# Block 1's inverse from sums by n mod 4, one accumulating transfer in block 3, and a new order of the work (SSM convolution and SwiGLU, one core)

## The chip, the cores and the metric

The kernel runs on 1 core of one Trainium2 chip. The metric is the device time of the program in microseconds, as the median of several runs. A profile of one execution lies beside it: it records every instruction of TensorE (PE, with its weight loads, PEld), VectorE (DVE), ScalarE (ACT) and GpSimd (POOL), and the DMA issues of the queues on SyncE (SP), ACT and POOL. Times in the profile run from the start of its span.

## The reference

The input is a sequence of 2048 rows of 640 channels. All inputs are bf16.

```
ks: k_shift[t] = sum over 4 taps of k[t - tap] * shift_k[tap]
kv = k_shift * v
y  = irfft(rfft(kv, 4096) * rfft(ssm_k, 4096))[0:2048] + kv * ssm_D   # a causal convolution, per channel
h  = x + layernorm(x) * y
out = h + (silu(n @ w_gate) * (n @ w_up)) @ w_down, with n = layernorm(h); 640 -> 1728 -> 640
```

## The kernel before

**Blocks.** The sequence is cut into 4 blocks of 512 rows, and each block lies in SBUF as 128 partitions of R = 4 rows of 640 channels (row n of a block is partition n // 4, place n mod 4). For every block j the kernel makes kv (`kv_of`), its spectrum X_j (`spectrum`, `transform`), the spectrum G_j of that part of the filter, and from it H_j (`window`). The spectra are products with constant cosine and sine matrices on PE (L375), taken out of PSUM by ACT (L364) or DVE (L367, `taken`). Block j's output spectrum A is the sum over i of X_i times H_(j-i), complex, which is DVE's work: `mac` with `first` set is six instructions (L719), and each further product is four pairs of a product (L746) and a sum into A (L747). A pair named in `ADDP` is a product alone (L741), and its sum is made by an accumulating transfer (`add_into`, L278), which the POOL queue issues. In the kernel before that is one pair of block 1.

**The inverse.** `inverse` (names i0 to i3) first makes `odd` = A_lo - A_hi (L823) and A_lo + A_hi (L826; block 2 by a transfer). Then it has two ways. In the plain way each of the four n mod 4 rows takes 4 constants against 2 halves of 320 columns: 8 matmuls (L878), 32 in all. In the way called "four" DVE first makes four more sums and differences of 128x1280 (L843, L848 write the parts for even rows, L858 those for odd rows), after which each row takes 2 constants: 4 matmuls, 16 in all. `SUM` names the blocks and spectra that go the second way; of the inverses these were i2 and i3. Each row is then multiplied with the normalised x (L807 or L804, then L892), added to x (L905, or by a transfer in blocks 1 and 2), and the second layernorm follows. The rows of h normalised again are turned on PE in block 0 (L926, copied by L928), and by a transposing DMA in the others (L919, from SP).

**The feed-forward part.** `ffn` of block j works on the turned rows hT of all 512 positions: 27 chunks of 5 matmuls of 128x512 (L1022) against weights that L959 loads, 320 KB at a time (`load_w`), with a SiLU (L1014) and a copy (L1012) on ACT and a product on DVE (L1016); then 12 groups of matmuls with w_down (L1110; 15 in the last block). The weights are loaded anew in every block. Each load stands on SP's queue, or on POOL's where the order says so.

**The order.** Nothing is ordered at run time. `plan.add` records every operation with its engine, and `ORDER` lists all of them by number; the engines, and the DMA queues of SP and POOL, get their instructions in this order. A number written as a negative (n stands as ~n) takes the operation's other engine: ACT for DVE, SP for POOL, or a DMA for one of ACT's copies. Buffers come from 12 slots called `big`, 8 called S, 5 called row and 4 PSUM tiles called ps, given out in the same order. So every engine and every queue waits at its own first instruction that isn't ready, and what stands behind it waits too.

**Names used below.** n_j are the sums of the first layernorm of block j (ACT L757, L796; POOL or DVE L764 to L789). k_j is the shifted key: of blocks 1 to 3 it is loaded by four transposing DMAs (L557) and copied within the tile T by three further copies, "puts" (L563 as a DMA, L565 on ACT), and PE multiplies it with the taps (L648); its product with v is ACT L664 and DVE L665, or DVE L658 alone. g_j is the filter block, turned on PE in blocks 0 to 2 (L471, copied by L473). m_ji is the product of X_i and H_(j-i) for block j; t_j is the second normalising and turning. f_j is the feed-forward part of block j; PE does f_j's chunks while DVE and ACT are at block j + 1.

Of the kernel before, what the change touches and what calls it, by code (L numbers as in the profile page):

```python
# [43 lines left out]
HTURN = (1, 3, 2)  # L44
GTURN = (3,)
KTURN = (1, 2, 3)
SUM = {'X3': 'four', 'i2': 'four', 'i3': 'four', 'G3': 'four'}
ADDP = {(1, 1): ((0, 1),)}
ADDINV = (2,)
WHOLE3 = False  # L50
WARMUP = (18, 16, 16)
# [17 lines left out]
TW = PAD + BLK  # L69
CUTS = ("X0", "G0", "m", "i")  # L70
ORDER = [
# [36 lines left out]
SLOTS = {'S': 8, 'big': 12, 'kT': 0, 'tT': 1, 'row': 5, 'sg': 0, 'co': 2, 'ps': 4, 'sm': 6}  # L108
HOME = {t: "big" for t in ("scr", "x", "ld", "t4", "hT", "wgu", "diag")} | {"o": "row", "ps_c": "ps", "ps_f": "ps"}
SPLIT = ((0,), (1,))  # L110
# [102 lines left out]
def kernel(ctx: ExitStack, tc: tile.TileContext, A_q, A_k, A_v, A_shift_k, A_ssm_k, A_ssm_D, B_x,  # L213
# [19 lines left out]
    def new(tag):  # L233
        return Buf(HOME.get(tag, tag), None, tag)
# [26 lines left out]
    def dve(ns, fn, r, w, holds=()):  # L261
        return plan.add("dve", ns, fn, r, w, holds)
# [82 lines left out]
    def bits(halves=(0, 1), cs=(0, 1, 2, 3), ws=(0, 1)):  # L345

        return frozenset((h, c, w) for h in halves for c in cs for w in ws)
# [31 lines left out]
    def wide(n, ws):  # L379
        return n if len(ws) == 2 else n // 2 + 75  # L380
# [10 lines left out]
    def transform(src, dst, pieces, minus=None, name=None):  # L391

        how = SUM.get(name, "sub")
        for ws in pieces:
# [418 lines left out]
    def inverse(A, x, n1, pieces=((0, 1),), minus=None, groups=(ROWS,)):  # L813
# [4 lines left out]
        for ws in pieces:  # L818
            if not minus:
# [10 lines left out]
                else:  # L830
                    dve(wide(1490, ws), low, [], [(A, bits(ws=ws))])
            four = not minus and SUM.get(f"i{plan.block}") == "four"
            if four:
# [404 lines left out]
    for j in range(1, NB):  # L1238
        def stage(name, j=j):
            plan.line(j, f"{name}{j}")  # L1240
# [23 lines left out]
        if last:  # L1264
            A = H[j]
            stage("m0")
            mac(A, X[0], H[j], True, at=(j, 0), adds=ADDP.get((j, 0), ()))
        stage("k")
# [4 lines left out]
        if not last:  # L1273
            stage("m0")
            A = Spec(new("S"))
            mac(A, X[0], H[j], True, at=(j, 0), adds=ADDP.get((j, 0), ()))
        for i in range(1, j + 1):
# [5 lines left out]
            else:  # L1283
                mac(A, X[i], H[j - i], False, adds=ADDP.get((j, i), ()), at=(j, i))
        stage("n")
# [45 lines left out]
```

## Time and profile before

| | |
|---|---|
| Time before, median of 3 runs | 261.34 us (261.23 to 261.5) |
| The profiled execution | 261.3 us |
| Its span | 259.6 us |
| Granted TensorE clock over the span | 1.0 |
| PE, DVE, ACT, POOL busy | 251.3, 198.6, 180.0, 97.0 us |
| DMA traffic | 45.38 MB, mean 175 GB/s |

The span runs from the first to the last recorded instruction, so 1.7 us of the execution's time lie around it. A row of a timeline is: start, length, engine, line, operation, output<-inputs, shapes, count, and in brackets the idle time of the engine just before it and what ended it. Rows of equal instructions are merged, so the length of a merged row over its count is a little above the distance from one to the next. A row of a group is: line, engine, operation, shapes, count, then busy time in all and the mean of one in ns, then the idle time before them.

### The profile page before, as it was taken

To read this page: it belongs to the slowest core of one execution; us is meant where nothing else is said; L and a number is where in the kernel's file an instruction comes from. 1 tells how busy PE (TensorE), PEld (TensorE's weight loads), DVE (VectorE), ACT (ScalarE), POOL (GpSimd) and SP (SyncE) were. 2 spreads that over 40 slices of the span, in tenths; PEclk is the share of its full clock that TensorE was granted. 3 is DMA by queue.
4 is the path that set the end of the run, shared out by engine and by line. 5 is a ranking of instruction groups with operands and counts; after the bars stand their busy time and mean duration, and the time that the engine had idled before them with its cause. 6 is when DMAs were issued, how large, how long until landed. Compare 5 with 4: busy or idle time off the path is not lost.

```text
span 259.6 us, 4700 instructions
## 1 busy us (share of the span) xinstructions
PE 251.3 (97%) x1803; PEld 154.2 (59%) x1818; DVE 198.6 (77%) x259; ACT 180.0 (69%) x297; POOL 97.0 (37%) x115
## 2 busy tenths in 40 slices
PE   8999899999998999999999999999999999999994
PEld 7967577654654477754465477544456764444663
DVE  4679999999998999999999999999998200004403
ACT  2899999999998998569855985655497134637200
POOL 7961300008914199926117962240951022000000
PEclk9999999999999999999999999999999999999999
DMA  6997999979999998999997965994498546000002
GB/s 218 403 251 119 289 252 340 280 115 279 247 238 168 182 217 204 190 191 201 214 231 110 299 151 107 198 238 130 100 215 255 101 77 70 8 0 0 13 15 76
DMA packets 64752, 45.38 MB, mean 175 GB/s; under 512 B 31014, under 2 KB 60267, under 8 KB 64731
## 3 DMA queue, kind: packets, MB, share of 16 engines
q1 hardware_dynamic: 58896, 32.96, 51.1%
q0 software_dynamic: 5824, 12.13, 24.9%
q8 instruction: 14, 0.23, 0.4%
q14 instruction: 8, 0.06, 0.1%
q10 hardware_dynamic: 10, 0.01, 0.0%
HBM read 30.01 MB, written 4.59 MB: 133 GB/s over the span
## 4 chain that ended last, share of the span: by engine, by line
PE 78%; ACT 9%; DMA 6%; DVE 2%; issue 2%; SPq 1%; ACTq 0%; DVEq 0%
PE ps L1022 40%; PE ps L1110 23%; PE ps L375 10%; DMA big<-in_B_w_up_dram 4%; PE ps L878 3%; DMA big<-in_A_q_dram 3%; ACT T L565 2%; ACT big L364 1%; ACT S L364 1%; PE ps L648 1%; ACT row L757 1%; ACT big L664 1%; ACT big L473 1%; ACT tT L1014 1%; DVE row L892 1%
## 5 line engine op out<-in xcount | busy, mean ns | idle before, releaser
L1022 PE MATMUL ps<-big,big 128*128 128x512 bf16 x525 | 119.9, 379 | 1.7 <-DMA big<-in_B_w_up_dram 0.8
L1022 PEld LDWEIGHTS <-big 128*128 128x128 bf16 x540 | 52.5, 98 | 61.1 <-DMA big<-in_B_w_up_dram 1.3
L1110 PE MATMUL ps<-wd,tT 128*128 128x320 bf16 (+1 forms) x416 | 60.3, 299 | 0.0
L1110 PEld LDWEIGHTS <-tT 128*128 128x128 bf16 x416 | 40.7, 98 | 16.3
L1016 DVE TENSOR_TENSOR tT<-tT,co 128x2048 bf16<-128x2048 bf16 x12 | 14.5, 1219 | 34.4 <-ACT tT L1014 32.4
L375 PE MATMUL ps<-big,WF 128*128 128x320 bf16 x240 | 39.1, 299 | 1.3 <-ACT big L364 1.0
L1012 ACT CAST co<-ps 128x1024 bf16<-128x1024 f32 x24 | 24.2, 1011 | 17.3 <-PE ps L1022 16.8
L747 DVE TENSOR_TENSOR S<-S,big 128x2560 bf16<-128x2560 bf16 x23 | 34.3, 1492 | 1.2 <-DMA S<-big 0.5
L746 DVE TENSOR_TENSOR big<-S,S 128x2560 bf16<-128x2560 bf16 x23 | 34.1, 1485 | 0.2
L375 PEld LDWEIGHTS <-WF 128*128 128x128 bf16 x240 | 23.1, 97 | 12.8 <-issue 2.3
L1014 ACT ACTIVATE tT<-ps 128x1024 bf16<-128x1024 f32 x24 | 24.5, 1029 | 8.8 <-PE ps L1022 8.7
L757 ACT ACTIVATE row<-big 128x640 bf16<-128x640 bf16 x32 | 23.5, 742 | 1.8 <-DMA big<-in_A_q_dram 1.1
L807 ACT ACTIVATE row<-big,sm 128x640 bf16<-128x640 bf16 x23 | 20.3, 922 | 3.8 <-POOL sm L789 2.8
L1117 POOL DMA_DIRECT2D out_dram<-row x12 | 11.8, 1010 | 29.2 <-ACT row L1116 29.1
L364 ACT CAST S<-ps 128x320 bf16<-128x320 f32 (+1 forms) x36 | 19.4, 583 | 0.3
L1116 ACT CAST row<-ps 128x640 bf16<-128x640 f32 x12 | 8.1, 691 | 14.2 <-PE ps L1110 13.2
L364 ACT ACTIVATE big<-ps 128x640 bf16<-128x640 f32 (+1 forms) x24 | 15.6, 696 | 0.7 <-PE ps L375 0.7
L278 POOL DMA_DIRECT2D big<-row x8 | 7.0, 919 | 22.9 <-DVE row L892 22.9
L892 DVE SCALAR_TENSOR_TENSOR row<-row,ps 128x640 bf16<-128x640 bf16 x16 | 12.8, 815 | 1.1 <-PE ps L878 0.9
L278 POOL DMA_DIRECT2D S<-big x2 | 2.5, 1266 | 26.3 <-DVE S L719 19.1
L719 DVE TENSOR_TENSOR big<-S,S 128x2560 bf16<-128x2560 bf16 (+1 forms) x10 | 12.2, 1218 | 0.1
L959 POOL DMA_DIRECT2D big<-in_B_w_gate_dram x8 | 9.1, 1137 | 8.1 <-PE ps L1022 7.8
(110 smaller groups left out, 330.4 us busy)
## 6 DMA issues: line engine op xcount, KB each, us to landing
big<-in_B_w_up_dram SPq DMA_DIRECT2D x17, 320.0 KB, 5.1
big<-in_B_w_gate_dram SPq DMA_DIRECT2D x16, 320.0 KB, 4.7
big<-in_A_ssm_k_dram SPq DMA_DIRECT2D x4, 640.0 KB, 9.2
big<-in_A_q_dram SPq DMA_DIRECT2D x4, 640.0 KB, 7.6
big<-in_A_v_dram SPq DMA_DIRECT2D x4, 640.0 KB, 6.9
big<-in_B_w_gate_dram POOLq DMA_DIRECT2D x8, 320.0 KB, 7.2
big<-in_B_w_up_dram POOLq DMA_DIRECT2D x7, 320.0 KB, 6.7
wd<-in_B_w_down_dram SPq DMA_DIRECT2D x1, 2080.0 KB, 12.2
```

The source lines that it names most:

```text
L364: (lambda: nc.scalar.activation(dst(), src(), ACT.Copy, scale=2.0)) if twice else (lambda: nc.scalar.copy(dst(), src())),
L375: nc.tensor.matmul(ap(ps)[:, h, 0:NH], w, ap(src)[:, r, h * NH:(h + 1) * NH], start=(first and i == 0), stop=(last and i == len(rs) - 1), ...
L746: nc.vector.tensor_mul(flat2(b), X.part(xs), H.part(hs))
L747: f(A.part(dst), A.part(dst), flat2(b))
L757: act(825, lambda r=r, junk=junk: nc.scalar.activation(ap(junk), ap(x)[:, r, :], ACT.Square, scale=D ** -0.5, accum_out=sm(s, 1)[:, r:r + ...
L807: nc.scalar.activation(ap(row), ap(x)[:, r, :], ACT.Identity, bias=sm(s, 5)[:, r:r + 1], scale=sm(s, 4)[:, r:r + 1])
L892: nc.vector.scalar_tensor_tensor(two(ap(t)), two(ap(t)), 1.0, half(ap(ps)), op0=ALU.mult, op1=ALU.mult, accum_out=sm(s, 0)[:, r:r + 1])
L1012: act(1010, lambda ps=ps: nc.scalar.copy(ap(co)[:, at:at + 2, :], ap(ps)), src, [(co, gi % 2)])
L1014: act(1010, lambda ps=ps: nc.scalar.activation(ap(tT)[:, c:c + 2, :], ap(ps), ACT.Silu), src, [done(range(c, c + 2), ROWS)])
L1016: dve(1220, lambda: nc.vector.tensor_mul(ap(tT)[:, c - 2:c + 2, :], ap(tT)[:, c - 2:c + 2, :], ap(co)), [co], [done(range(c - 2, c + 2), R ...
L1022: nc.tensor.matmul(ap(ps)[:, i, :], ap(w)[:, k, off:off + P], ap(hT)[:, k, :], start=(k == 0), stop=(k == KT - 1))
L1110: nc.tensor.matmul(ap(ps)[:, hf, to:to + n], t, ap(wd)[:, c, col + (hf - hs[0]) * NH:col + (hf - hs[0]) * NH + n], start=(c == order[0]), ...
```

## The change

Three constants change; no function does.

```diff
-SUM = {'X3': 'four', 'i2': 'four', 'i3': 'four', 'G3': 'four'}
-ADDP = {(1, 1): ((0, 1),)}
+SUM = {'X3': 'four', 'i2': 'four', 'i3': 'four', 'G3': 'four', 'i1': 'four'}
+ADDP = {(1, 1): ((0, 1),), (3, 2): ((0, 1),)}
...
-ORDER = [0, 2, 31, 1, 4, 5, 7, 10, 6, ...
+ORDER = [0, 2, 4, 1, 5, 31, 6, 7, 10, ...
```

- Block 1's inverse goes the way called "four": 16 of its 32 matmuls go, and four DVE instructions of 128x1280 come.
- In block 3 the sum of one of the four pairs of X_2 and H_1 (that of X's first part with H's second part, into A's second part) leaves DVE, and an accumulating transfer of 640 KB on POOL's queue makes it.
- The whole order is another. 16 instead of 20 loads stand on POOL's queue: of f1's 3 instead of 6, of f2's 3 instead of 4, of f3's 4 instead of 5; and SP's queue takes 5 more. Of k2's three puts two are DMAs of POOL's queue and one is ACT's copy (before: one of SP's queue, two of ACT's). Of k3's one put goes from POOL's queue to SP's.
- Some operations change engines: of the four products of k3 with v one goes from DVE alone (L658) to ACT and DVE (L664, L665); one in k0 the other way. A copy of g2 (L473) goes from DVE to ACT, one of g1 from ACT to DVE. Of the second normalising in block 3, three rows instead of one are ACT's, and one instead of three DVE's.

The core of the function that both ways of the inverse share, with what the new constant switches on:

```python
four = not minus and SUM.get(f"i{plan.block}") == "four"
if four:
    ...
    dve(wide(820, ws), lambda r02=r02: r02(nc.vector.tensor_add, 0), [(A, h0)], [(A, bits((1,), (0, 1), ws))])
    dve(wide(820, ws), lambda r02=r02: r02(nc.vector.tensor_sub, 2), [(A, h0)], [(A, bits((1,), (2, 3), ws))])
    ...
        for sub in (True, False):
            ...
            dve(820 if len(ws) == 2 else 485, lambda pair=pair, sub=sub: pair(sub), [odd], [(A, bits((0,), rows, ws))])
...
elif four:
    terms = [(ap(WI)[:, 2 * c, r, :], ap(A)[:, 1 - r % 2, r // 2 * 2 + (c ^ (lo // 2)), :]) for c in range(2)]
else:
    terms = [(ap(WI)[:, c, r, :], ap(odd)[:, c ^ lo, :] if r % 2 else ap(A)[:, 0, c ^ lo, :]) for c in range(4)]
```

73 rows, old and new, of the table ORDER are left out of this document.

## The prediction, made before the changed kernel ran

> **What bounds the kernel now.** I read the page first, then the chain of waits, then the busy time in stretches of 10 us, then the timeline where those pointed.
>
> ```profile
> PE 251.3 (97%) x1803; PEld 154.2 (59%) x1818; DVE 198.6 (77%) x259; ACT 180.0 (69%) x297; POOL 97.0 (37%) x115
> ...
> PE 78%; ACT 9%; DMA 6%; DVE 2%; issue 2%; SPq 1%; ACTq 0%; DVEq 0%
> ```
>
> PE carries 78% of the chain that ends last. But the 77% of DVE is a mean over two very different parts, as the stretches show (PE, PEld, DVE, ACT, POOL busy, clock, DMA share, GB/s):
>
> ```profile
> 30.00:40.00 10.00, 9.77 (x121) 7.36 (x120) 9.93 (x20) 9.49 (x19) 0.17 (x1) 1.00 1.09 266
> 40.00:50.00 10.00, 9.54 (x95) 6.92 (x96) 9.62 (x22) 10.00 (x20) 0.41 (x1) 1.00 1.15 299
> ...
> 160.00:170.00 10.00, 9.95 (x62) 5.88 (x61) 9.89 (x8) 6.31 (x13) 3.12 (x3) 1.00 0.87 172
> ...
> 180.00:190.00 10.00, 9.95 (x48) 4.52 (x48) 9.77 (x9) 5.63 (x9) 7.66 (x6) 1.00 0.34 77
> ...
> 210.00:220.00 10.00, 9.95 (x52) 4.95 (x52) 0.00 (x0) 3.92 (x5) 2.67 (x4) 1.00 0.50 53
> ```
>
> Up to 50 us PE, DVE and ACT are all full; up to 190 us DVE is as full as PE; behind 210 PE runs alone, the clock is 1.0 and nothing can be won there but PE's own work. So there are two runners, PE and DVE, that must meet at block 3's inverse, and a gain on one alone counts only as far as the other lets it. They meet here:
>
> ```profile
> 188.14 1.56 DVE L843 TENSOR_TENSOR S<-S 128x1280 bf16<-128x1280 bf16 x2
> ...
> 189.83 0.71 PE L878 MATMUL ps<-S,WI 128*128 128x320 bf16 x4
> ...
> 201.71 5.17 SPq L919 DMA_TRANSPOSE big<-row  x4
> ...
> 211.53 3.83 PE L1022 MATMUL ps<-big,big 128*128 128x512 bf16 x16
> ```
>
> The first of the two L843, which the first inverse row reads, ends at 188.14 + 0.78 = 188.92. PE begins that row at 189.83: DVE is 0.9 us early, no more. The turned rows of block 3 land 2.6 us after the fourth L919 is issued at 205.7, so at 208.3, and PE begins f3 at 211.5: 3.2 us to spare.
>
> ```profile
> L919 SPq DMA_TRANSPOSE big<-row x12: 1198/1228/1439, 101.6 to 205.7; - x12
> ...
> DMA to landing us min/median/max: 2.6/2.6/2.7
> ```
>
> From that first row to f3, PE has 211.53 - 189.83 = 21.7 us of its own work. The sum below is therefore made in two columns, PE and DVE up to block 3's first inverse row, then one.
>
> **The change part by part.** *(a) 16 matmuls of block 1's inverse go.*
>
> ```profile
> 73.67 2.34 PE L878 MATMUL ps<-big,WI 128*128 128x320 bf16 x16
> 75.84 2.32 PE L1022 MATMUL ps<-big,big 128*128 128x512 bf16 x10
> ...
> 81.11 1.25 PE L1022 MATMUL ps<-big,big 128*128 128x512 bf16 x4 [0.78 <-DMA big<-in_B_w_up_dram]
> ```
>
> Sixteen take 75.84 - 73.67 = 2.17 us from start to start (0.136 each). PE: -2.2.
>
> *(b) DVE's own sum.*
>
> ```profile
> L843 DVE TENSOR_TENSOR S<-S 128x1280 bf16<-128x1280 bf16 x4 | 3.1, 818 | 0.0
> L747 DVE TENSOR_TENSOR S<-S,big 128x2560 bf16<-128x2560 bf16 x23 | 34.3, 1492 | 1.2 <-DMA S<-big 0.5
> L658 DVE TENSOR_TENSOR big<-ps,big 128x640 bf16<-128x640 f32 x5 | 4.0, 813 | 1.5 <-PE ps L639 1.5
> L665 DVE TENSOR_TENSOR big<-big,big 128x640 bf16<-128x640 bf16 x11 | 5.1, 484 | 0.1
> L473 DVE COPY big<-ps 128x640 bf16<-128x640 bf16 x5 | 2.3, 486 | 1.1 <-PE ps L471 1.1
> L804 DVE TENSOR_SCALAR row<-big,sm 128x640 bf16<-128x640 bf16 x9 | 3.7, 439 | 0.0
> ```
>
> Block 1's inverse adds four of 128x1280: 4 x 0.818 = +3.3. Block 3's sum goes to the transfer: -1.5. One product of k3 becomes L665: 0.484 - 0.813 = -0.3. Behind block 0's second norm, the copy of g2 (0.5) and one row of h0 (0.4) go to ACT: -0.9. That is +0.6 up to block 3's inverse, none of it hidden, DVE being full. Bounds: 0 to +1.5, since the -0.9 falls away if ACT is late with the last piece of G1.
>
> *(c) ACT is the engine on which f0's start hangs, and the new order loads it.* In the chain it runs unbroken from 38 to 48.5 us, up to the last copy of block 0's turned rows (L928).
>
> ```profile
> 8.85 0.74 ACT L757 ACTIVATE row<-big 128x640 bf16<-128x640 bf16 x1 [1.07 <-DMA big<-in_A_q_dram]
> ...
> 35.63 0.69 ACT L473 COPY big<-ps 128x640 bf16<-128x640 bf16 x1 [0.38 <-PE ps L471]
> ...
> 42.38 1.93 ACT L364 ACTIVATE big<-ps 128x640 bf16<-128x640 f32 x3
> 44.14 1.94 ACT L364 CAST S<-ps 128x640 bf16<-128x640 f32 x3
> ...
> 48.23 1.41 ACT L928 COPY big<-ps 128x640 bf16<-128x640 bf16 x2
> ...
> 49.70 1.24 PE L1022 MATMUL ps<-big,big 128*128 128x512 bf16 x4
> L757 ACT ACTIVATE row<-big 128x640 bf16<-128x640 bf16 x32 | 23.5, 742 | 1.8 <-DMA big<-in_A_q_dram 1.1
> L807 ACT ACTIVATE row<-big,sm 128x640 bf16<-128x640 bf16 x23 | 20.3, 922 | 3.8 <-POOL sm L789 2.8
> ```
>
> Counted in the two programs from the last two copies of kv of block 1 to the fourth L928: 13 instructions before, 17 after. The four more are a copy of g2 (0.6), a row of h0 (20.3/23 = 0.88), and a piece each of X1 and G2 ((44.14 - 42.38)/3 = 0.59): +2.6 us. Ahead of that stand three more sums of n1 (3 x 0.73) and one row fewer (-0.88), +1.3, which the idle 1.07 at the start and the idle 0.38 can swallow; I let them. So f0 begins at 49.7 + 2.6 = 52.3. PE isn't idle for all of that: two more pieces of G2 stand ahead of f0, 8 matmuls or 1.1 us. PE: +1.5. Bounds: +0.5 (1 us of the four more also falls into small gaps) to +2.8 (nothing swallowed).
>
> *(d) Weights and queues in f0.* PE's one wait for a DMA is the 0.78 us at 81.11 above. The new order loads the last chunk's weights much earlier, but it now asks for w_up of the fifth group behind a load of f1, and for that of the sixth when its slot is freed 9 us ahead of use:
>
> ```profile
> 71.61 9.45 DMA big<-in_B_w_up_dram
> ...
> big<-in_B_w_up_dram SPq DMA_DIRECT2D x17, 320.0 KB, 5.1
> big<-in_B_w_gate_dram POOLq DMA_DIRECT2D x8, 320.0 KB, 7.2
> T<-T POOLq DMA_DIRECT2D x3, 321.2 KB, 7.4
> ```
>
> In this stretch a load takes 9.45 us, so those arrive within half a microsecond of PE. Between -0.8 (the wait gone) and +1.0 (one load late by that); I take -0.3. k2's second put is a DMA behind the first: two times 7.4 us from the transposes' landing near 53.5 give 68.5, and PE wants it at about 71: hidden, but by 2.5 us only.
>
> By the rule of the Trainium skill (DMA: Bandwidth & Descriptors, "Issuing engines are not separate DMA queues") moving weights from POOL to SP saves only time on the issuing sequencer. The rows of this page differ: the same 320 KB land after 5.1 us from SP and after 7.2 from POOL. By the rule the five moved loads are worth nothing, by the rows about 2 us each, and as they land tens of us ahead of use in both orders the sum is the same.
>
> *(e) The accumulating transfer, and what stands before it.* X_3's lower half is itself made by such a transfer, issued when L443 is done. Before, four pairs of m_32, 11.9 us, lay between L443 and the first product that reads it. Now it is the lone product (1.5) and two pairs (2 x 2.97): 7.4 us.
>
> ```profile
> 158.70 1.49 DVE L443 TENSOR_TENSOR S<-S,big 128x2560 bf16<-128x2560 bf16 x1
> ...
> 160.77 1.25 POOL L278 DMA_DIRECT2D S<-big  x1 [7.26 <-issue]
> DMA to landing us min/median/max: 6.8/6.8/6.8
> DMA to landing us min/median/max: 9.9/9.9/9.9
> ```
>
> It was issued 0.58 us behind L443's end and landed 6.8 us later: 7.4 behind, exactly what is left. The other transfer of this form, near 59.5 us, took 9.9 (and DVE waited 0.5 for it); with that DVE would wait 3.1. The trace has no two of them in a row, as the change issues them. Between 0 and +3.1; I take +0.5, near the row of the same transfer. The new transfer itself is asked for only 13.4 us after L443, some 11 after its issue: hidden.
>
> **Sum.** DVE's first part for block 3's inverse is ready at 188.9 + 0.6 + 0.5 = 190.0. PE arrives at 189.8 + 1.5 - 2.2 - 0.3, plus 1.1 as one chunk more of f2 stands ahead of that row now: 189.9. So both are there at 190.0. From there PE has 21.7 - 1.1 = 20.6 us to f3: 210.6 instead of 211.5. Block 3's turned rows took 208.3 - 188.9 = 19.4 us from the same point; three of the four rows are now scaled on ACT (0.88 instead of 0.44, the first one counts: +0.4), which gives 209.8 and no wait. f3 and the end are unchanged. **-0.9 us**: 261.3 of the profiled execution becomes **260.4**; the median of 261.34 agrees with that execution.
>
> **The rivals.** *PE's work was never the price (no difference).* If nothing of the early ACT work is swallowed, f0 begins 3.9 late; PE (+2.8 - 2.2 - 0.3 + 1.1) comes at 191.2 and f3 at 211.8: 261.6. The same end comes if DVE is 0.9 later at the inverse: PE's 2.2 us would be given back there as a wait. For it: DVE gets longer, not shorter, and is full. Against it: 0.9 us of room was there before.
>
> *The accumulating transfers come late (slower).* At a landing of 9.9 us, DVE waits 3.1 ahead of the first product with X_3, is at the inverse at 189.5 + 3.1 = 192.6, and f3 begins at 213.2: +1.7, 263.0. It decides from 8.8 us on (190.9 at the inverse gives 211.5). For it: 9.9 us was seen once, and the other accumulating transfer follows at once. Against it: the one measured in this place took 6.8. The Trainium skill (SBUF — State Buffer, "Who interferes with whom") says that GpSimd and a DVE instruction in a two-port mode exclude each other for the whole instruction, so that descriptors which GpSimd writes wait for DVE. The trace can't show that apart, as DVE was full around both transfers.
>
> *Everything in f0 is on time (faster still).* The 0.78 us wait gone and f0 only 1.6 late: PE comes at 188.4, but DVE not before 189.5, so f3 at 210.1: 259.9. DVE's column is the floor, so even this is only 0.5 more.
>
> **How the numbers follow.** Forecast (-0.5 to -1.5 us) and the last rival: 0.40 and 0.10. No difference: 0.22. Late transfers, or in the same way a late put or weight in f0: 0.28. A measurement of this kernel can tell about 0.2%, 0.5 us, from no change. So faster 0.50, same 0.22, slower 0.28. The range reaches from 259.4 (DVE at its lower bound with the last rival) to 262.6, leaving out the last part of the late transfers.
>
> **What would show it.** Right: 16 L878 in block 1 instead of 32; f0's first chunk at 52 +- 0.7 us; PE without a wait at block 3's first inverse row, which starts near 190; f3 near 210.6. Wrong: a wait of DVE for a DMA into S ahead of the first product with X_3 (e); a wait of PE on L843 or L858 in block 3 of over 0.5 us; f0's first chunk before 51 or after 53.5; PE waits on weights or T between 55 and 82 us that add up to more than 1 us.

## The result, and the profile after

The changed kernel took **265.7 us** (median of 6 runs, 262.4 to 266.8) against 261.3 of the kernel before: ratio 1.013, 95% interval 1.008 to 1.018. The ratio leaves out the execution of 266.8 us, which counts as slow. A second set of 6 gave 265.6 and 1.017 (1.014 to 1.021). The forecast was 260.4 with a range from 259.4 to 262.6. The profiled execution took 264.92 us, its span is 262.9.

The page of the changed kernel (all line numbers are one higher than before):

```profile
PE 249.6 (95%) x1786; PEld 152.2 (58%) x1802; DVE 199.8 (76%) x258; ACT 180.8 (69%) x300; POOL 98.2 (37%) x112
L376 PE MATMUL ps<-big,WF 128*128 128x320 bf16 x240 | 38.3, 298 | 4.9 <-ACT S L365 2.9
```

PE is busy 1.7 us less, near the 2.2 of the 16 matmuls that are gone, and still the span is 3.3 us longer: PE stands still more. The group of the spectra's matmuls stood 1.3 us before (L375); now it is 4.9, and 2.9 of it is one wait for ACT. The stretches show where (us, then PE, PEld, DVE, ACT, POOL busy, clock, DMA share, GB/s):

```profile
0.00:53.00 53.00, 47.47 (x513) 36.70 (x514) 45.58 (x94) 46.85 (x102) 18.65 (x44) 1.00 0.96 259
53.00:100.00 47.00, 46.74 (x323) 26.55 (x326) 46.42 (x46) 42.85 (x69) 29.87 (x17) 1.00 1.08 232
100.00:108.00 8.00, 5.12 (x39) 3.55 (x38) 4.60 (x4) 4.68 (x7) 2.96 (x5) 1.00 0.51 90
108.00:190.00 82.00, 81.50 (x516) 45.66 (x522) 81.28 (x75) 55.67 (x84) 41.17 (x41) 1.00 0.85 175
190.00:200.00 10.00, 9.11 (x49) 4.60 (x48) 9.15 (x13) 7.72 (x10) 1.17 (x2) 1.00 1.08 299
```

From 100 to 108 us **PE, DVE and ACT all stand**, for about 3 us each, and 0.9 us more are lost at 190 to 200. Everywhere else behind 53 us PE is full. The two places in the timeline, ACT and PE:

```profile
97.95 0.71 ACT L365 CAST S<-ps 128x640 bf16<-128x640 f32 x1
103.32 0.92 ACT L808 ACTIVATE row<-big,sm 128x640 bf16<-128x640 bf16 x1 [4.67 <-POOL sm L790]
104.15 0.67 ACT L365 CAST S<-ps 128x640 bf16<-128x640 f32 x1
104.87 0.70 PE L376 MATMUL ps<-big,WF 128*128 128x320 bf16 x4 [2.88 <-ACT S L365]
...
196.33 1.24 PE L1023 MATMUL ps<-big,big 128*128 128x512 bf16 x5 [0.89 <-ACT tT L1033]
```

ACT stands 4.67 us before the first row of h1 of block 1 (L808), which needs that block's second norm from GpSimd (L790). Behind the row stands the last copy of X_2 out of PSUM (L365, 104.15), for which ACT was free at 98.7; PE waits for its PSUM, and DVE for X_2 (3.35 us). Before, the same copy stood behind the same row, and ACT waited there too, but for 0.98 us only:

```profile
100.61 0.92 ACT L807 ACTIVATE row<-big,sm 128x640 bf16<-128x640 bf16 x1 [0.98 <-POOL sm L789]
101.43 0.67 ACT L364 CAST S<-ps 128x640 bf16<-128x640 f32 x1
```

The copy ended at 102.10, and DVE, done with its product at 102.04, took X_2 up at 102.14. So the order of before had no room left here, but lost next to nothing. The norm ended at 100.6 before and at 103.3 now, though GpSimd began it 6 us earlier. GpSimd's timeline of before and of after:

```profile
91.50 1.39 POOL L766 TENSOR_SCALAR sm<-sm 128x4 f32<-128x4 f32 x1
92.97 1.40 POOL L767 TENSOR_TENSOR sm<-sm,sm 128x4 f32<-128x4 f32 x1
...
100.10 0.47 POOL L789 TENSOR_TENSOR sm<-sm 128x4 f32<-128x4 f32 x1
```
```profile
85.56 11.60 POOL L767 TENSOR_SCALAR sm<-sm 128x4 f32<-128x4 f32 x1
97.24 1.40 POOL L768 TENSOR_TENSOR sm<-sm,sm 128x4 f32<-128x4 f32 x1
...
103.09 0.20 POOL L790 TENSOR_TENSOR sm<-sm 128x4 f32<-128x4 f32 x1
```

The first instruction of the norm, four numbers in each partition, is given **11.6 us**. By its record it waits for no semaphore. DVE's timeline over the same time:

```profile
85.89 1.48 DVE L720 TENSOR_TENSOR S<-S,S 128x2560 bf16<-128x2560 bf16 x1
87.29 0.88 DVE L666 TENSOR_TENSOR big<-big,big 128x640 bf16<-128x640 bf16 x2
88.09 1.48 DVE L720 TENSOR_TENSOR big<-S,S 128x2560 bf16<-128x2560 bf16 x1
...
94.17 1.48 DVE L720 TENSOR_TENSOR S<-S,big 128x2560 bf16<-128x2560 bf16 x1
95.58 1.48 DVE L747 TENSOR_TENSOR big<-S,S 128x2560 bf16<-128x2560 bf16 x1
97.09 1.49 DVE L748 TENSOR_TENSOR S<-S,big 128x2560 bf16<-128x2560 bf16 x1
```

From 85.89 on every DVE instruction starts 0.07 to 0.08 us before the record of the one ahead of it ends (85.89 + 1.48 = 87.37, the next at 87.29). The first gap is at 97.06 to 97.09: L748 needs what L747 writes. GpSimd's instruction ends at 97.16.

### The profile page after: what moved, and what is told of

It reads as the page before. It is cut to its first block, busy times and chain, and to the rows that moved or that the text cites. A ratio compares the mean times of both kernels' runs of the same rounds, so it can differ in the third digit from the quotient of the medians.

```text
span 262.9 us, 4664 instructions
## 1 busy us (share of the span) xinstructions
PE 249.6 (95%) x1786; PEld 152.2 (58%) x1802; DVE 199.8 (76%) x258; ACT 180.8 (69%) x300; POOL 98.2 (37%) x112
## 4 chain that ended last, share of the span: by engine, by line
PE 58%; ACT 1%; issue 1%; DVE 0%; ACTq 0%
PE ps L1023 33%; PE ps L1111 20%; PE ps L376 2%; PE ps L879 2%; PE ps L649 1%; ACT tT L1015 0%; ACT co L1013 0%; ACT S L365 0%; ACT tT L1033 0%; DVE row L1128 0%; ACT row L808 0%; ACTq L365 0%
## 5 line engine op out<-in xcount | busy, mean ns | idle before, releaser
L1023 PEld LDWEIGHTS <-big 128*128 128x128 bf16 x540 | 52.3, 98 | 61.8 <-issue 1.2
L1111 PE MATMUL ps<-wd,tT 128*128 128x320 bf16 (+2 forms) x416 | 60.9, 299 | 0.0
L376 PE MATMUL ps<-big,WF 128*128 128x320 bf16 x240 | 38.3, 298 | 4.9 <-ACT S L365 2.9
L748 DVE TENSOR_TENSOR S<-S,big 128x2560 bf16<-128x2560 bf16 x22 | 32.8, 1492 | 0.8
L747 DVE TENSOR_TENSOR big<-S,S 128x2560 bf16<-128x2560 bf16 x22 | 32.7, 1484 | 0.1
L808 ACT ACTIVATE row<-big,sm 128x640 bf16<-128x640 bf16 x25 | 22.6, 924 | 6.3 <-POOL sm L790 4.7
L758 ACT ACTIVATE row<-big 128x640 bf16<-128x640 bf16 x32 | 23.6, 740 | 1.3 <-DVE big L906 0.8
L365 ACT CAST S<-ps 128x320 bf16<-128x320 f32 (+1 forms) x36 | 20.4, 596 | 1.0 <-PE ps L376 0.8
L1035 DVE TENSOR_TENSOR tT<-tT,co 128x512 bf16<-128x512 bf16 x4 | 1.7, 414 | 23.6 <-ACT tT L1033 23.6
L365 ACT ACTIVATE big<-ps 128x640 bf16<-128x640 f32 (+1 forms) x24 | 15.4, 702 | 0.4 <-PE ps L376 0.4
L797 ACT ACTIVATE row<-big 128x640 bf16<-128x640 bf16 x16 | 12.0, 751 | 2.7 <-DMA big<-row 2.7
```

The costliest lines, as they stand in the source:

```text
L365: (lambda: nc.scalar.activation(dst(), src(), ACT.Copy, scale=2.0)) if twice else (lambda: nc.scalar.copy(dst(), src())),
L376: nc.tensor.matmul(ap(ps)[:, h, 0:NH], w, ap(src)[:, r, h * NH:(h + 1) * NH], start=(first and i == 0), stop=(last and i == len(rs) - 1), ...
L747: nc.vector.tensor_mul(flat2(b), X.part(xs), H.part(hs))
L748: f(A.part(dst), A.part(dst), flat2(b))
L758: act(825, lambda r=r, junk=junk: nc.scalar.activation(ap(junk), ap(x)[:, r, :], ACT.Square, scale=D ** -0.5, accum_out=sm(s, 1)[:, r:r + ...
L808: nc.scalar.activation(ap(row), ap(x)[:, r, :], ACT.Identity, bias=sm(s, 5)[:, r:r + 1], scale=sm(s, 4)[:, r:r + 1])
```

## The experiments

**Theory A**: DVE's run without a gap keeps GpSimd out; the norm is late; ACT, in order, stands before a row with PE's and DVE's next work behind it. **Theory B**: the 11.6 us were a chance of one execution. **Theory C**: the stall only shows a loss that would come anyway.

**1. The changed kernel again.**

> The changed kernel once more, unchanged. Theory A: PE's idle 2.9 us at 102 us comes from GpSimd, whose first instruction of block 1's second norm (L767) is kept out for 11.6 us while DVE runs products without a gap; ACT then stands 4.7 us before a row of h1 (L808), with the last copy of X_2 (L365) queued behind it. If DVE's order alone decides that, L767 again takes over 9 us, ACT again stands over 3 us and the time is 264 to 266. Theory B: the 11.6 us were a chance of that one execution; then L767 takes 1 to 3 us here and the time is near 262.

265.6 us. The first instruction came in at once here, and the second was held, up to the same place (GpSimd, then DVE):

```profile
85.73 0.24 POOL L767 TENSOR_SCALAR sm<-sm 128x4 f32<-128x4 f32 x1
86.06 11.29 POOL L768 TENSOR_TENSOR sm<-sm,sm 128x4 f32<-128x4 f32 x1
```
```profile
95.81 1.47 DVE L747 TENSOR_TENSOR big<-S,S 128x2560 bf16<-128x2560 bf16 x1
97.32 1.49 DVE L748 TENSOR_TENSOR S<-S,big 128x2560 bf16<-128x2560 bf16 x1
```

The held instruction ends at 97.35, DVE's product at 97.28. PE waited 2.6 us. Theory B falls.

**2. The sum moved ahead.** DVE's numbers in ORDER; 475 is the pair. With it 473 goes ahead, and 470 goes behind 377:

```diff
-442, 451, 470, 445, 368, 473, 472, 377, 474, 475, 476
+442, 451, 473, 445, 368, 475, 377, 470, 472, 474, 476
```

> The changed kernel with DVE's order changed between 84 and 98 us: the first pair of a product (L747) and the sum that needs it (L748) stands five instructions earlier; nothing else is moved. Before it DVE's instructions start 0.07 us ahead of the end of the one before them, at this pair there is a gap of 0.03 us. Theory A: L767 on GpSimd ends within 0.2 us of the first such gap, near 92.5 instead of 97.2, the norm is done near 99, ACT stands under 1 us, and the time is 261.5 to 262.5. Rival (L767 is held by something that has nothing to do with DVE, such as its own code or its data): it ends at 97 us again, and the time is 264 to 266.

**262.1 us**, 3.5 less than the changed kernel; against before 1.004 (1.002 to 1.006). GpSimd, then DVE:

```profile
86.18 6.76 POOL L768 TENSOR_TENSOR sm<-sm,sm 128x4 f32<-128x4 f32 x1
```
```profile
91.40 1.47 DVE L747 TENSOR_TENSOR big<-S,S 128x2560 bf16<-128x2560 bf16 x1
92.91 1.49 DVE L748 TENSOR_TENSOR S<-S,big 128x2560 bf16<-128x2560 bf16 x1
```

DVE's product ends at 92.87, the held instruction at 92.94, and the stall at 102 us is gone.

**3. The gap alone.** DVE's order stays; two tiny instructions come in behind number 451:

```diff
+nc.vector.tensor_add(ap(gap1), ap(root), ap(root))
+nc.vector.tensor_add(ap(gap2), ap(gap1), ap(gap1))
```

> The changed kernel in its own order, with two tiny sums on DVE added behind the third product of k2 (near 88.2 us); the second needs the first, so there is a gap between them; together about 0.35 us. Theory A (GpSimd comes in only where DVE leaves a gap): the instruction of block 1's second norm that was kept out for 11 us ends within 0.3 us of this pair, near 88.8 instead of 97.2; the norm is done by 97, ACT and PE don't stand at 102 us, and the time is 261.5 to 262.8, like that of the run with the sum moved ahead (262.1). Rival (moving the sum helped for another reason, such as the order of the products themselves): the instruction still ends at 97 and the time is 264.5 to 266.

262.4 us, 1.003 of before (0.9995 to 1.006). GpSimd, then DVE:

```profile
86.82 2.40 POOL L768 TENSOR_TENSOR sm<-sm,sm 128x4 f32<-128x4 f32 x1
```
```profile
88.28 0.88 DVE L666 TENSOR_TENSOR big<-big,big 128x640 bf16<-128x640 bf16 x2
89.09 0.14 DVE L1302 TENSOR_TENSOR gap<-root 128x4 f32<-128x4 f32 x1
89.27 0.16 DVE L1303 TENSOR_TENSOR gap<-gap 128x4 f32<-128x4 f32 x1
```

Two instructions whose results nothing uses took 3.2 us off, and DVE's products kept their order: the pair ends the hold, and the loss goes with it. That it is the gap inside the pair is not shown. The held instruction ends at 89.22, ahead of that gap (89.23 to 89.27) and 0.06 behind the end of L666 (89.16); in experiment 2 the same instruction ended 0.07 behind the DVE instruction ahead of the gap. By this it came in ahead of the first tiny instruction, at a place without a gap.

**4. The norm on DVE.**

```diff
-LN2POOL = (1, 2)
+LN2POOL = (2,)
```

> The changed kernel with block 1's second norm on DVE instead of GpSimd: ten small instructions, 2.0 us by the rows of block 0's norm, and up to 0.9 us in which DVE waits for the last square sum at 91.9. Theory A: ACT and PE no longer stand at 102 us; DVE loses 2 to 3 us by the norm instead of 3.3 by the stall, so the time is 262 to 264.5, under the changed kernel's. Theory C (the stall was not what costs): the 2 to 3 us of DVE come on top, 266 to 268.

263.2 us, 1.009 (1.005 to 1.012). The stall is gone, and DVE's own longer work shows in its place: PE waits 1.0 us for L1035 and 0.9 us for L844. Theory C falls with this and the two runs before.

**5. Rows later on ACT**, two of them or all four (313, 311, 309, 315 are the rows):

```diff
-455, 313, 463, 311, 641, 309, 315, 643
+455, 463, 641, 313, 311, 309, 315, 643
...
+455, 463, 641, 643, 637, 385, 400, 313, 311, 309, 315
```

> The changed kernel with two of the four rows of h1 of block 1 (L808) moved on ACT behind the last copy of X_2 and the first of G_3 (L365). Theory A (ACT's order behind a late norm makes the loss): PE's 2.9 us and DVE's 3.3 us at 102 us go, the rows are not later than they were, so block 3's first inverse row comes about 3 us earlier and the time is 261.5 to 262.5. Theory C (the stall only shows a loss that DVE or f1 would take later anyway): PE's wait moves to block 1's turned rows or to the inverses, and the time stays within 1 us of the changed kernel's, 264 to 266.

269.2 us, slower. With two rows moved, PE and DVE ran on at 102 us, so GpSimd went on finding DVE busy: the norm ended at 106.0 instead of 103.3, and the next copies stood behind the rows for longer. PE's clock fell too (0.50 from 112 to 116 us), so the time holds more than the wait.

```profile
106.05 3.36 ACT L808 ACTIVATE row<-big,sm 128x640 bf16<-128x640 bf16 x4 [3.23 <-POOL sm L790]
110.03 0.70 PE L376 MATMUL ps<-big,WF 128*128 128x320 bf16 x4 [3.34 <-ACT big L365]
```

> The changed kernel with all four rows of h1 of block 1 (L808) moved on ACT behind the two output copies and the pieces of X_2 and G_3 that stand up to 110.4 us there; DVE and GpSimd as in the changed kernel, so the norm is late as before, or later (106 us in the run with two rows moved, where DVE never stood still). If a late norm costs only through the copies that queue behind the rows on ACT: PE isn't stopped at 102 us, the rows are ready near 110, their transposes land near 113, PE waits under 1.5 us for them at f1, and the time is 261.5 to 263. If the late norm costs by itself: f1 waits 3 us or more for the rows, and the time is 264 to 267.

274.3 us. Here the last two rows waited for two of the five row buffers, which the output copies ahead of them had taken in another order, and which the transposes set free. Those landed up to 11.1 us after their issue here, against a median of 2.6:

```profile
117.37 0.92 ACT L808 ACTIVATE row<-big,sm 128x640 bf16<-128x640 bf16 x1 [8.75 <-DMA big<-row]
122.04 1.23 PE L376 MATMUL ps<-big,WF 128*128 128x320 bf16 x4 [11.48 <-ACT big L365]
```

Both expectations missed. They can't tell whether a late norm costs without a queue behind it, since each made a new queue; they do show that the wait only moves as long as something stands behind a row on ACT.

**6. The 0.9 us at 196 us.** On the run with the sum moved ahead, two inverse rows of block 3 (716, 717) go ahead of the half chunk (802) that waits for PSUM:

```diff
-719, 801, 802, 716, 717, 806
+719, 801, 716, 717, 802, 806
```

> The run with the sum moved ahead (262.1), and on PE two rows of block 3's inverse (L879) ahead of a half chunk of f2 that waited 0.9 us for ACT (L1033). If that wait is what is left between the changed kernel and the kernel before, it goes and the time is 261.0 to 261.5. Rival (DVE isn't ready for these rows earlier): the 0.9 us come back as a wait of L879 for DVE, and the time stays at 262.

**260.8 us**, 0.9975 (0.9947 to 1.0003). It is the best version found; that it beats the kernel before is not shown, as the interval reaches 1. Its stretches behind 53 us:

```profile
53.00:100.00 47.00, 47.00 (x327) 26.57 (x326) 46.59 (x46) 43.17 (x70) 27.53 (x19) 1.00 1.04 219
100.00:108.00 8.00, 8.00 (x61) 5.77 (x59) 7.80 (x7) 6.98 (x10) 1.35 (x2) 1.00 0.78 144
```

From 53 us to the last groups of matmuls PE has no idle time left.

**7. The accumulating transfer undone**, on the run with the sum moved ahead:

```diff
-ADDP = {(1, 1): ((0, 1),), (3, 2): ((0, 1),)}
+ADDP = {(1, 1): ((0, 1),)}
```

> The run with the sum moved ahead (262.1), with block 3's product sum back on DVE in place of the accumulating transfer. DVE gets 1.5 us longer ahead of block 3's inverse. In the run with the sum moved ahead, DVE was done 0.7 us before PE asked for the first row. Theory (the transfer is worth what PE would otherwise wait): 0.5 to 1.0 us slower, 262.6 to 263.1. Rival (DVE's end there hangs on something other than its own work): no change, 262.

261.6 us, 1.003 (0.9999 to 1.005): not slower. My 0.7 us of room was read from the second of the two L844; the row needs the first. In the run with the sum moved ahead that one is ready at 188.19 + 0.78 = 188.97, and PE asks near 190.7, so 1.5 us more of DVE fit.

**8. The head** (everything up to f0), all on the kernel of experiment 6. First, PE's fill matmuls (41) ahead of those that wait for the first load (55, 59, 57):

```diff
-55, 59, 57, 41
+41, 55, 59, 57
```

> The run with the two inverse rows ahead (260.8), and on PE the 16 fill matmuls of block 0 (L1152, 1.1 us) ahead of the matmuls that wait for the first load (L472), as the kernel before has them; there they cover the wait. If PE's start in the head counts, X_0 begins up to 1 us earlier and 0.5 to 1.0 us are won where the load comes late: 259.8 to 260.4. Rival (ACT is the bound in the head): no change, 260.5 to 261.

261.1 us, 0.999 (0.996 to 1.001): no change. Then the order of the kernel before for the first 288, 320 and 350 of ORDER's numbers, the rest as it was:

```diff
-ORDER = [0, 2, 4, 1, 5, 31, 6, 7, 10, ...
+ORDER = [0, 2, 31, 1, 4, 5, 7, 10, 6, ...
```

> The kernel with the two inverse rows ahead on PE, and with the order of the kernel before for everything up to the first chunk of f0. f0 begins at 49.7 instead of 53.3 us, with three pieces of G_2 and X_1 less behind it. By the sum of PE's idle time up to 60 us (5.6 us in the changed kernel, 3.2 before) PE should win up to 2.4 us; DVE's work is the same as in the changed kernel. If the head is what costs: 259.5 to 260.5. Rival (DVE is the floor from 60 to 190 us, the head's gain is given back as waits of PE): within 0.5 us of the run with the rows ahead.

> The run with the two inverse rows ahead (260.8), with the order of the kernel before for all that stands there up to the last piece of G_2 (57.6 us), so that f0's first chunks and the pieces of G_2 keep the order that they had among each other. From 53.5 us on that run's PE is idle for 0.02 us in all, so only the head can still give something: its PE is idle 3.5 us up to f0 (2.2 before). If the head's order is what costs there: f0 begins at 49.7, no wait of 2.6 us as in the run with the head of before alone, and the time is 259.3 to 260.3. Rival (what the head wins is given back where DVE or ACT is the floor, as in that run): 260.5 to 262.5.

> The same with the order of the kernel before up to the three pairs of m_11 (67 us), just ahead of block 1's inverse. If the head's order is what costs: 259.3 to 260.3. Rival (ACT's and DVE's later work fits the changed order's head only): 260.5 to 262.5.

262.4, 262.5 and 263.8 us (1.003, 1.007 and 1.012). f0 began up to 4 us earlier, but PE then waited in it for ACT, 2.6 and 1.5 us in the first of them, 2.4 and 3.0 in the others. The second, in PE's timeline and its waits:

```profile
49.65 1.24 PE L1023 MATMUL ps<-big,big 128*128 128x512 bf16 x4
```
```profile
PE ps L1023 <- ACT tT L1015: 2.4, 1, 2.4
```

PE's clock fell as well in the last two (0.67 from 68 to 72 us, 0.50 from 76 to 80 us). Of the first's twelve executions three took 260.8 to 261.0 us, like experiment 6, and nine 262.2 to 262.9. A head joined from two orders makes waits of its own, so what the changed head costs by itself isn't measured by these; they show PE's gain in the head given back as waits for ACT.

## Why the prediction was wrong

The sign was wrong. First chunk or matmul of the same work, from the timelines of after and of the run of experiment 6:

```profile
53.31 1.24 PE L1023 MATMUL ps<-big,big 128*128 128x512 bf16 x4
116.01 2.32 PE L1023 MATMUL ps<-big,big 128*128 128x512 bf16 x9
193.65 0.71 PE L879 MATMUL ps<-S,WI 128*128 128x320 bf16 x4
215.32 1.89 PE L1023 MATMUL ps<-big,big 128*128 128x512 bf16 x7
```
```profile
113.31 2.97 PE L1023 MATMUL ps<-big,big 128*128 128x512 bf16 x13
190.89 0.71 PE L879 MATMUL ps<-S,WI 128*128 128x320 bf16 x4
211.52 4.70 PE L1023 MATMUL ps<-big,big 128*128 128x512 bf16 x21
```

f3 was forecast for 210.6 and began at 215.3, 4.7 late: 2.9 by the stall at 102 us, 1.1 behind the first inverse row (0.9 of it the wait for ACT), and 0.7 by the time of that row.

- **The step that failed is the sum's form: two columns, PE and DVE, up to block 3's inverse.** It put nothing between f0 and 190 us for GpSimd, and took ACT for free behind 50 us. In its place the runs showed a wait of 2.9 us of PE, because block 1's norm ended at 103.3 instead of 100.6. The row of the trace of before that spoke against it is quoted above: ACT already stood 0.98 us for GpSimd's norm at 100.6, with the last copy of X_2 behind that row, so there was no room there at all. The new order kept that and put a run of eleven DVE instructions without a gap over the norm. The rivals named late transfers, a late head and a late DVE; none named a late norm.
- **(a)** was right. From f0's first chunk to f1's, PE took 113.66 - 49.70 = 64.0 before and 62.7 now; less the stall of 2.9, that is 4.1 less. The parts named were 2.2 (16 matmuls), 1.1 (8 matmuls of G_2 moved ahead of f0) and the wait of 0.78.
- **(b)** was too high. DVE, forecast 1.1 later at block 3's inverse with (e), is at the same place without the stall: 188.97 in the run of experiment 2, against 188.92 before. Its small waits before 100 us went, among them 0.5 us for a transfer and 0.7 us for PE; I had counted only work.
- **(c)** had the right mechanism and was 1.0 us short: f0 at 53.3 instead of 52.3, outside the 52 +- 0.7 that was to show it right, but inside the bound (3.9 late, 53.6). Almost nothing of ACT's early work was swallowed. PE also waited 1.15 us for the first load, since its fill matmuls now stand behind that wait, but moving them changed nothing (experiment 8). f0 doesn't follow that wait either: it began at 53.3 in experiment 2, where the wait was 1.9 us, and at 53.7 in experiment 6 without one. ACT stood for only about 1 us between 9 us and f0, so ACT is the bound there.
- **(d)** was right: PE waits for no weights between 55 and 100 us, and k2's second put landed at 68.4, with PE's first product at 72.3 and no wait. PE's wait of 0.55 us for T in the changed kernel is at 38.2, for block 1's key. By the two traces 10 instead of 15 weight loads stand on POOL's queue; what that is worth by itself no run measured.
- **(e)** was right that nothing waits. The two transfers in a row landed 5.9 and 8.9 us after their issue and DVE never stopped for them. But the transfer in place of DVE's sum gained nothing that these runs show: experiment 7.
- **PE and DVE meet at 190** held without the stall: the first inverse row is at 190.9 in experiment 6, and from there to f3 it took 20.6 us, as forecast.

The order brought 3.8 us of waits (2.9 and 0.9) for which the sum had no column. With them removed, the change comes to -0.6 us with an interval that touches zero, against the forecast -0.9. The trace of experiment 6 doesn't show that gain: f3 begins at 211.52, as before (211.53). Single executions differ by as much, though: in the trace of the run with the fill moved f3 begins at 210.84. In experiment 6 DVE was ready early at block 3's inverse (188.41 + 0.78 = 189.2), but PE came at 190.9 instead of 189.9: about what (c) was short by. One execution of the changed kernel took 262.4 us; there is no trace of it, and whether GpSimd came in earlier there stays open.

## What to carry to other kernels

Give every engine that some chain passes through a column, the lightly loaded ones too: a small norm on GpSimd that ends just in time is a bound, and a wait of 1 us on an in-order queue in the trace of before is the place to look at first when an order changes. Then ask what stands behind the waiting instruction in the new order. Where DVE is full, a GpSimd instruction's length is not its own: the same kind, 128x4, took 0.2 to 11.6 us here. Look at what DVE runs beside it; in this kernel two tiny DVE instructions at that place, the second needing the first, ended the hold.

## What the runs showed of the hardware

**GpSimd next to a full DVE.** In all twelve traces of the new order with block 1's norm on GpSimd, one of its first two instructions (128x4) was held: for 11.3 to 11.6 us in four traces with DVE's order of the changed kernel around it, 6.7 to 7.0 us in seven with the sum moved ahead, 2.4 us with the tiny pair. In eleven it ended 0.06 to 0.10 us behind the DVE instruction ahead of the first gap of 0.03 us; with the pair, 0.06 behind the one ahead of the pair. The Trainium skill (SBUF — State Buffer, "Who interferes with whom") says that DVE and GpSimd share a pair of ports under an exclusive lock, and that a DVE instruction with two inputs in SBUF contends with a GpSimd instruction that reads SBUF. The trace agrees in that the instructions here are of these forms and GpSimd's ended just behind one of DVE's. It shows more: GpSimd can be held over eleven DVE instructions. But a gap is not needed for it to come in: in the trace of before, 9 of GpSimd's 29 instructions of 128x4 behind 50 us ended within 0.1 us of a DVE end without a gap. And in the run with the tiny pair, a later instruction of the norm came in between two DVE instructions that had kept the first one out in the changed kernel: it ended at 93.84, DVE's at 93.78, and DVE's next had begun at 93.70.

```profile
93.02 0.82 POOL L786 TENSOR_TENSOR sm<-sm 128x4 f32<-128x4 f32 x1 [3.52 <-ACT row L758]
92.30 1.48 DVE L720 TENSOR_TENSOR S<-S,big 128x2560 bf16<-128x2560 bf16 x1
93.70 1.48 DVE L720 TENSOR_TENSOR S<-S,S 128x2560 bf16<-128x2560 bf16 x1
```

What tells the two cases apart isn't settled.

**A stall of PE can cost twice.** In the second profile of the changed kernel PE's clock fell behind the stall; in the first, with a stall about as long, it didn't. Stretches of the second:

```profile
104.00:106.00 2.00, 1.19 (x7) 0.77 (x7) 1.21 (x1) 2.00 (x4) 0.00 (x0) 0.83 0.28 56
106.00:108.00 2.00, 2.00 (x9) 1.14 (x8) 1.97 (x3) 1.79 (x3) 0.00 (x0) 0.50 0.89 81
108.00:110.00 2.00, 2.00 (x13) 1.34 (x12) 2.00 (x2) 0.87 (x2) 0.19 (x1) 0.82 0.67 116
```

At 0.50 PE did about half as much (9 matmuls in 2 us, against 17 at the same place in the first profile): f1 began 1.6 us later than in the first profile, 0.2 of which it was late ahead of the stall. Of the changed kernel's twelve executions the six with a mean clock of 0.992 to 0.994 took 266.0 to 266.8 us, and five of the six at 1.0 took 264.7 to 265.4. After the idle 11.5 us of the run with four rows moved the clock stood at 0.50 from 116 to 126 us. The Trainium skill (TensorE: Matmul & The Clock Gate, "What's actually happening") says that a window without activity halves the clock until a busy window has passed, and that the windows run free of the program; the halving and the difference between two nearly equal stalls agree with that. The Trainium skill gives about 3.4 us for a window there; here PE stood for only 2.6 us before the clock fell, so that length does not come out of these runs, and the windows themselves no run here shows.
